# Decode attention with a gated MLP: the K and V loads move from SyncE's DMA queue to GpSimd's, each as a single packet for an engine

## Chip, core and metric

One NeuronCore of a Trainium2 chip runs the whole kernel in one launch. The metric is the device time of one execution in microseconds; lower is better. The core has five engines, which run their own instruction streams and meet at semaphores: TensorE (PE), VectorE (DVE), ScalarE (ACT), GpSimd (POOL) and SyncE (SP). Sixteen DMA engines move data between HBM and the on-chip memory (SBUF); SP, ACT and POOL can issue transfers to them.

## What is computed

One decode step for a batch of 4: layer norm, attention of one query against a cache of 8192 keys and values for each of 32 heads, then layer norm and a gated MLP, both with a residual.

```python
q = (layernorm(x) @ wq).reshape(B, 1, H, Dh)          # B=4, D=512, H=32, Dh=128
scores = einsum("bhqd,bhkd->bhqk", q, k_cache) * Dh ** -0.5
o = einsum("bhqk,bhkd->bhqd", softmax(scores), v_cache)   # Sk=8192
h = x + o.reshape(B, 1, H * Dh) @ wo
n = layernorm(h)
out = h + (sigmoid(n @ w_gate) * (n @ w_up)) @ w_down      # F=1792
```

All tensors are bf16. The K and V caches are 268 MB each, read once; everything else is small beside them.

## The kernel before

**Groups.** The 128 pairs of batch entry and head are worked on in NG = 32 groups of four heads of one batch entry. A group's K is one load of 128 partitions x 64 KB (8.4 MB), its V another. The tile KV has three slots of this size, through which 64 loads pass in turn: K0 in slot 0, K1 in slot 1, V0 in slot 2, K2 in slot 0, V1 in slot 1, K3 in slot 2 and so on.

**One group.** VectorE transposes K in place, in eight pieces (`transpose_k`, L332). TensorE multiplies each piece by the query vectors in Lq (`scores`, L342). VectorE and ScalarE make the softmax (`softmax`, L352 to L375); the step that closes the scores' use of K is the transpose at L357, and its token is `t_a5[g]`. TensorE then multiplies by V (`pv`, L385), one group later, and VectorE takes the result out of PSUM (`extract`, L412 to L415), two groups later, between the second and the third piece of the next transposes; its token is `t_ox[g]`. GpSimd has two small steps for each group: `fill_q` (L282) lays the next group's query vectors into Lq, and `keep_o` (L286) copies the result away. A group's first transpose waits for its K load, for `fill_q` and for the softmax step before.

**Loads and their waits.** `load_k(g)` waits for `t_ox[g-3]`, because its slot held V of group g-3; `load_v(g)` waits for `t_a5[g]`, because its slot held K of group g. The first ones differ: K0 waits for nothing, K1 for two matmuls on x (which lies in slot 1), K2 for `t_a5[0]`, and V0 for the projection of the queries (`t_qp`, L253), because slot 2 first holds the weight wq. All of these are issued by SyncE (L292 and L301, the last V at L299), in this order: wq (L181), K0, K1, V0, K2, V1, K3, V2 and so on, then the weights wo, w_gate, w_up (behind `t_a5[31]`) and w_down (behind the pv of group 30). x is loaded from ScalarE's queue (L180).

**The start.** wq has to land before the 128 matmuls at L253 can run; out of them come, through VectorE (L257, L269) and 16 small matmuls (L263), the query vectors, which `fill_q(0)` needs. GpSimd first clears and fills constants (L184 to L198).

**Loops and semaphores.** TensorE's and VectorE's streams are hardware loops of 10 turns over three groups each; ScalarE, GpSimd and SyncE run straight through. Inside the loops a wait must be on a constant, so these semaphores are counted down: a load adds 16 to `sl0` to `sl2` (K) or `v0` to `v2` (V), and the waiting engine subtracts 16 again (`take` in `emit`). The last V has a semaphore of its own, `vl`, that is only counted up. `fill` (L434) is work without a result that keeps TensorE's clock up in the last stage.

Of the kernel before, what the change touches and what calls it, by code (L numbers as in the profile page):

```python
# [11 lines left out]
class _Prog:  # L12
# [28 lines left out]
    def emit(self, eng, fn, waits=(), incs=1, key=None, take=(), keep=True):  # L41

        todo = self._waits(eng, waits)
        assert not (todo and self.looped), (eng, todo)
        key = key or eng
        tok = self.token(key, incs) if incs else None

        def run(e):
            for k, v in todo:
                e.wait_ge(self.sems[k], v)  # L50
            for k, v in take:
                e.wait_ge(self.sems[k], v).then_inc(self.sems[k], -v)  # L52
            made = fn(e)
            made = made if isinstance(made, list) else [made]
            if incs:
                assert len(made) == incs
                for m in made:
                    m.then_inc(self.sems[key], 1)

        if keep:  # L60
            self.ops[eng].append(run)
        return tok
# [26 lines left out]
def bass_sequential_preLN__mha_block_cached__glu_gated_glu__decode_kernel(  # L89
# [20 lines left out]
    SLOT = 4 * S * DH // 128  # L110
# [5 lines left out]
    prog = _Prog()  # L116
    emit = prog.emit

    with ExitStack() as es:
# [3 lines left out]
        def raw(t):  # L123
            return t.tensor if hasattr(t, "tensor") else t
# [31 lines left out]
        def kv(slot, off, inner, p0=0, np_=128):  # L156
            return bass.AP(raw(KV), p0 * KVROW + slot * SLOT + off, [[KVROW, np_], *inner])
# [10 lines left out]
        FY = (bank[1], FA)  # L168

        keys = ["sp", "act", "dve", "pool", "pe", "x", "out", "cs", "wq", "wo0", "wo1", "wg", "wu", "wd0", "wd1", "wd2", "wd3",  # L170
                "sl0", "sl1", "sl2", "vl", "v0", "v1", "v2", "tp", "pt", "ex", "dv", "sc", "pv", "lq"]
        for k in keys:
            prog.sems[k] = es.enter_context(nc.semaphore("s_" + k))

        dram_k = lambda g: A_k_cache[g % B, 4 * (g // B):4 * (g // B) + 4, :, :].rearrange(
            "h (p r) d -> (h p) (r d)", p=32)
        dram_v = lambda g: A_v_cache[g % B, 4 * (g // B):4 * (g // B) + 4, :, :].rearrange(
            "h (p r) d -> (h p) (r d)", p=32)
# [95 lines left out]
        t_v, t_et, t_pv, t_ox = {}, {}, {}, {}  # L274
        t_a5, t_oc = {}, {}

        def fill_q(g):
            m, b = g // B, g % B
            dst = bass.AP(raw(Lq), 15, [[4 * LW, 128], [LW, 4], [32, 4]])
            src = bass.AP(raw(q_all), m * 4 * B + b, [[128, 128], [B, 4], [0, 4]])  # L280
            msk = bass.AP(raw(mask), 0, [[4, 128], [0, 4], [1, 4]])
            emit("pool", lambda e: e.tensor_tensor(dst, src, msk, ALU.mult),  # L282
                 [t_q, t_mk, t_lq0, t_a5.get(g - 1), t_oc.get(g - 3)], key="lq")

        def keep_o(g):
            t_oc[g] = emit("pool", lambda e: e.tensor_copy(OT[:, g // B, :, g % B], OTs[:, g % 3, :]), [t_ox[g]])  # L286

        def load_k(g):
            i = max(2 * g - 1, 0)
            kslot[g] = slot = i % 3  # L290
            w = [] if g == 0 else [t_xT] if g == 1 else [t_a5[0]] if g == 2 else [t_ox[g - 3]]
            prog.dma("sp", f"sl{slot}", lambda e: e.dma_start(kv(slot, 0, [[1, SLOT]]), dram_k(g)), w)  # L292

        def load_v(g):
            last = g == NG - 1
            vslot[g] = slot = 0 if last else (2 * g + 2) % 3
            w = [t_ox[g - 2]] if last else [t_a5[g]] if g else [t_qp]
            if last:
                t_v[g] = [prog.dma("sp", "vl", lambda e: e.dma_start(kv(slot, 0, [[1, SLOT]]), dram_v(g)), w)] * 4  # L299
            else:  # L300
                t_v[g] = [prog.dma("sp", f"v{slot}", lambda e: e.dma_start(kv(slot, 0, [[1, SLOT]]), dram_v(g)), w)] * 4  # L301

        t_w = {}
        kslot, vslot = {}, {}
# [154 lines left out]
                return ins  # L459
            return emit("pe", f, waits)  # L460

        fill_q(0)
        load_k(0)
        load_k(1)
        load_v(0)
        TURNS = (NG - 2) // 3
        assert 2 + 3 * TURNS == NG
        for g in range(NG):
# [13 lines left out]
            if g > 1:  # L482
                keep_o(g - 2)
                if g + 1 < NG:
                    load_k(g + 1)
                else:
                    load_v(g)
# [3 lines left out]
            if 0 < g < NG - 1:  # L491
                load_v(g)
# [106 lines left out]
        def o_half(u):  # L599
# [3 lines left out]
        key, v = prog.dma("act", "out", lambda e: e.dma_start(  # L603
            out.rearrange("b s d -> (b s) d"), kv(0, 0, [[1, D]], 0, B)), [t_o])
# [33 lines left out]
```

## Time and profile before

| | |
|---|---|
| median of 3 runs | 1277.1 us (1276.98 to 1277.11) |
| the profiled execution | 1277.14 us, of which its span 1275.6 us |
| instructions in the span | 10932 |
| read from HBM | 550.77 MB, 432 GB/s over the span |
| granted TensorE clock, mean | 0.918 of full speed |

The profile records one execution. Times in its rows are microseconds from the start of the span. In a timeline row the first number is the start, the second the length; then follow engine, line of the kernel, operation, output<-inputs, the count of instructions merged into the row, and in brackets the idle time of the engine before it and what ended that. SPq and ACTq are the issue of a DMA by SyncE and ScalarE: the row's length is that of the issue, not of the transfer. A row with "KB" or a number after "x1," gives the time from the issue to the landing of the transfer. A row that begins with two times and a colon is one stretch: its length, the busy time and instruction count of PE, PE's weight loads, DVE, ACT and POOL, the granted clock, the DMA engines' busy share and GB/s. In a queue row stand its packets, megabytes and the time that they took as a share of 16 engines; q1 is SyncE's queue, q10 ScalarE's, and q8 and q14 fetch instructions.

### The profile page before, as it was taken

Reading aid. Unit: us, or ns where it says so; the run is one execution under the profiler, and the core shown is the slowest. Engines: PE = TensorE matmul, PEld = TensorE weight load, DVE = VectorE, ACT = ScalarE, POOL = GpSimd, SP = SyncE. Lnnn points to the kernel's source line nnn. Section 1 sums busy time; section 2 is a strip of 40 time slices with the busy share of each in tenths; the row PEclk is TensorE's granted clock in tenths of the full one; section 3 lists DMA queues with packets and bytes.
Section 4 is the critical chain, followed back from the end, with each engine's and each line's share of the span. In section 5 each row is a group of like instructions: output and inputs, shape, how many; then the busy total and the mean of one; then the engine's idle time right before and its main releaser. Section 6 shows DMA issues by size and latency. Waiting matters only on the chain. (4 is left out here: it accounts for less than half of the span.)

```text
span 1275.6 us, 10932 instructions
## 1 busy us (share of the span) xinstructions
PE 1001.2 (78%) x4450; PEld 409.7 (32%) x4450; DVE 701.8 (55%) x737; ACT 85.2 (7%) x202; POOL 22.6 (2%) x88
## 2 busy tenths in 40 slices
PE   1598777779777788777798777797777897777888
PEld 1233323333233333223333233333233332333334
DVE  0865665446655446654456654456554466544562
ACT  0000000000000000000000000000000000000010
POOL 1000000000000000000000000000000000000000
PEclk9899888899888898888998888998888998888989
DMA  9999999999999999999999999999999999999998
GB/s 420 434 425 434 427 444 432 430 438 427 442 434 430 438 427 444 432 432 436 427 444 432 432 436 434 438 432 434 434 434 438 432 436 432 436 436 430 440 430 371
DMA packets 10669, 550.95 MB, mean 432 GB/s; under 512 B 1176, under 2 KB 1440, under 8 KB 1824
## 3 DMA queue, kind: packets, MB, share of 16 engines
q1 hardware_dynamic: 10640, 550.77, 99.8%
q8 instruction: 8, 0.13, 0.0%
q14 instruction: 5, 0.04, 0.0%
q10 hardware_dynamic: 16, 0.01, 0.0%
HBM read 550.77 MB, written 0.00 MB: 432 GB/s over the span
## 5 line engine op out<-in xcount | busy, mean ns | idle before, releaser
L332 DVE STREAM_TRANSPOSE KV<-KV 128x2048 uint32<-128x2048 uint32 x256 | 568.6, 2279 | 379.1 <-DVEq L52 379.1
L342 PE MATMUL PS<-KV,Lq 128*128 128x512 bf16 x2048 | 543.6, 417 | 258.2 <-PEq L52 257.5
L385 PE MATMUL PS<-KV,PT 128*128 128x512 bf16 x1984 | 433.2, 379 | 0.0
L342 PEld LDWEIGHTS PS<-KV,Lq 128*128 128x128 bf16 x2048 | 199.8, 104 | 601.4 <-issue 442.7
L385 PEld LDWEIGHTS PS<-KV,PT 128*128 128x128 bf16 x1984 | 193.8, 98 | 234.5
L358 ACT ACTIVATE E_sb<-PS,TS 128x512 bf16<-128x512 f32 x32 | 22.0, 688 | 1124.6 <-DVE TS L357 1124.6
L352 DVE TENSOR_REDUCE TS<-PS 128x1 f32<-128x512 f32 x32 | 22.1, 692 | 70.4 <-DVEq L52 70.4
L369 ACT ACTIVATE PT<-ET 32x256 bf16<-32x256 bf16 x128 | 52.9, 413 | 30.8 <-DVE ET L361 28.5
L361 DVE STREAM_TRANSPOSE ET<-E_sb 128x512 bf16<-128x512 bf16 x32 | 22.8, 711 | 30.7 <-DVEq L52 30.7
L412 DVE STREAM_TRANSPOSE OX<-PS 128x512 f32<-128x512 f32 x31 | 20.9, 675 | 8.6 <-DVEq L52 8.6
L282 POOL TENSOR_TENSOR Lq<-q_all,mask 128x16 bf16<-128x16 bf16 x32 | 8.4, 263 | 575.0 <-DVE TS L357 563.4
L286 POOL COPY OT<-OTs 128x4 bf16<-128x4 bf16 x30 | 5.8, 192 | 622.3 <-DVE OTs L415 622.3
L434 PE MATMUL PS<-identf 128*128 128x512 f32 (+3 forms) x30 | 13.3, 551 | 0.0
L253 PE MATMUL PS<-xnT,KV 128*128 128x4 bf16 x128 | 3.6, 166 | 9.4 <-DMA KV<-in_A_wq_dram 9.4
L353 DVE STREAM_TRANSPOSE TS<-TS 128x32 f32<-128x32 f32 x32 | 6.8, 211 | 5.1 <-DVEq L52 0.6
L357 DVE STREAM_TRANSPOSE TS<-TS 128x32 f32<-128x32 f32 x32 | 6.8, 211 | 4.7
L374 DVE STREAM_TRANSPOSE TS<-TS 128x32 f32<-128x32 f32 x32 | 6.8, 211 | 4.7
L415 DVE TENSOR_SCALAR OTs<-Or,small 128x4 bf16<-128x4 f32 x30 | 6.9, 229 | 4.5 <-DVEq L52 1.4
L373 DVE COPY TS<-small 128x32 f32<-128x32 f32 x32 | 5.8, 182 | 6.2 <-DVEq L52 3.0
L355 DVE TENSOR_SCALAR TS<-small 128x32 f32<-128x32 f32 x32 | 5.8, 181 | 4.8 <-DVEq L52 0.2
L414 DVE TENSOR_REDUCE Or<-OX 128x4 f32<-128x16 f32 x31 | 5.6, 179 | 4.5
L354 DVE TENSOR_REDUCE small<-TS 128x1 f32<-128x16 f32 x32 | 5.4, 170 | 4.7
(87 smaller groups left out, 78.1 us busy)
## 6 DMA issues: line engine op xcount, KB each, us to landing
KV<-in_A_wq_dram SPq DMA_DIRECT2D x1, 4096.0 KB, 12.4
KV<-in_A_wo_dram SPq DMA_DIRECT2D x2, 2048.0 KB, 22.1
KV<-in_B_w_gate_dram SPq DMA_DIRECT2D x1, 1792.0 KB, 28.2
KV<-in_B_w_up_dram SPq DMA_DIRECT2D x1, 1792.0 KB, 32.0
KV<-in_B_w_down_dram SPq DMA_DIRECT2D x1, 1024.0 KB, 24.2
KV<-in_A_k_cache_dram SPq DMA_DIRECT2D x32, 32.4
KV<-in_A_v_cache_dram SPq DMA_DIRECT2D x32, 34.3
KV<-in_B_w_down_dram SPq DMA_DIRECT2D x1, 512.0 KB, 25.0
```

Of the source, the lines that this page charges most:

```text
L282: emit("pool", lambda e: e.tensor_tensor(dst, src, msk, ALU.mult), [t_q, t_mk, t_lq0, t_a5.get(g - 1), t_oc.get(g - 3)], key="lq")
L332: emit("dve", lambda e: e.transpose(v, v), key="tp", take=take, keep=keep)
L342: ins = e.matmul(S_b[0], Lq[:, hp, 15 - s:15 - s + 128], rhs, start=(s == 0 and hp == 0), stop=(s == NS - 1 and hp == 3))
L352: dv(lambda e: e.tensor_reduce(TS[:, 0, 0:1], S_b[0], AX.X, ALU.max), [t_ts0] if g == 0 else [], [("sc", 1)])
L353: dv(lambda e: e.transpose(TS[:, 1, :], TS[:, 0, :]))
L358: emit("act", lambda e: e.activation(E_sb[:, :], S_b[0], ACT.Exp, bias=TS[:, 3, 0:1], scale=SCALE, accum_out=TS[:, 4, 0:1]), [t_a5[g]], ke ...
L361: t_et[g] = dv(lambda e: e.transpose(ET[:, :], E_sb[:, :]), take=[("ex", 1)], key="dve")
L369: emit("act", lambda e, dst=dst, src=src: e.activation(dst, src, ACT.Copy), [t_et[g], t_pt0 if g < NG - 1 else t_ptl], key="pt")
L385: ins = e.matmul(O_b, PT[:, u3, off:off + 128], rhs, start=(j == 0 and rl == 0), stop=(j == 3 and rl == NS - 1))
L412: emit("dve", lambda e: e.transpose(OX[:, :, :].rearrange("p (r i) x -> p r i x", r=4), src), w, key="dv", take=take, keep=keep)
L415: t_ox[g] = emit("dve", lambda e: e.tensor_scalar(dst, Or[:, :], small[:, 2 + g % 3:3 + g % 3], None, op0=ALU.mult), take=[("dv", 1)], kee ...
L434: ins = e.matmul(bk[:, 0:cols], identf[:, :], bass.AP(raw(identf), 0, [[128, 128], [0, cols // 128], [1, 128]]), start=True, stop=True, sk ...
```

## The change

The K and V loads are issued by GpSimd, through a new helper `stream`, with `single_packet=True`. Each adds 16 to a new semaphore of its slot, `g0` to `g2`, that is only counted up. For each such load SyncE's stream gets a wait for that count, followed by an addition of 16 to the old semaphore, `sl` or `v`, which the loops count down as before. The last V adds to `vl` itself. The loads of x and of all weights stay where they were. In GpSimd's stream the order becomes: constants, K0, K1, `fill_q(0)`, V0, `fill_q(1)`, K2, `fill_q(2)`, V1, and then for each group `keep_o`, K, `fill_q`, V. SyncE's stream is wq, the waits, and the later weights. Nothing changes on TensorE, VectorE and ScalarE.

```diff
-                "sl0", "sl1", "sl2", "vl", "v0", "v1", "v2", ...
+                "sl0", "sl1", "sl2", "vl", "g0", "g1", "g2", "v0", "v1", "v2", ...
...
+        def stream(slot, key, src, w):
+            own = key if key == "vl" else f"g{slot}"
+            own, v = prog.dma("pool", own, lambda e: e.dma_start(
+                kv(slot, 0, [[1, SLOT]]), src, single_packet=True), w)
+            if own != key:
+                prog.ops["sp"].append(lambda e: e.wait_ge(prog.sems[own], v).then_inc(prog.sems[key], 16))
+            return own, v
+
         def load_k(g):
...
-            prog.dma("sp", f"sl{slot}", lambda e: e.dma_start(kv(slot, 0, [[1, SLOT]]), dram_k(g)), w)
+            stream(slot, f"sl{slot}", dram_k(g), w)
...
             if last:
-                t_v[g] = [prog.dma("sp", "vl", lambda e: e.dma_start(kv(slot, 0, [[1, SLOT]]), dram_v(g)), w)] * 4
+                t_v[g] = [stream(slot, "vl", dram_v(g), w)] * 4
             else:
-                t_v[g] = [prog.dma("sp", f"v{slot}", lambda e: e.dma_start(kv(slot, 0, [[1, SLOT]]), dram_v(g)), w)] * 4
+                stream(slot, f"v{slot}", dram_v(g), w)
...
-        fill_q(0)
         load_k(0)
         load_k(1)
+        fill_q(0)
         load_v(0)
```

More of the change, by code (lines that the diff above doesn't have):

```diff
@@ L170, in bass_sequential_preLN__mha_block_cached__glu_gated_glu__decode_kernel @@
         keys = ["sp", "act", "dve", "pool", "pe", "x", "out", "cs", "wq", "wo0", "wo1", "wg", "wu", "wd0", "wd1", "wd2", "wd3",
-                "sl0", "sl1", "sl2", "vl", "v0", "v1", "v2", "tp", "pt", "ex", "dv", "sc", "pv", "lq"]
+                "sl0", "sl1", "sl2", "vl", "g0", "g1", "g2", "v0", "v1", "v2", "tp", "pt", "ex", "dv", "sc", "pv", "lq"]
         for k in keys:
```

## The prediction

> **What bounds the kernel now.** I read the page's totals first, then the DMA queues, then one turn of the loop, then the two ends.
>
> ```profile
> span 1275.6 us, 10932 instructions
> PE 1001.2 (78%) x4450; PEld 409.7 (32%) x4450; DVE 701.8 (55%) x737; ACT 85.2 (7%) x202; POOL 22.6 (2%) x88
> DMA  9999999999999999999999999999999999999998
> q1 hardware_dynamic: 10640, 550.77, 99.8%
> ```
>
> No compute engine is busy over 78%, while one DMA queue keeps all 16 engines at work for 99.8% of the span. The next rows are one turn in the middle, group 16 or so: the totals of the turn, its DMA packets, the landing times of its two loads, and the instructions around their issue (start, length, engine, line).
>
> ```profile
> 600.00:638.62 38.62, 31.45 (x129) 12.81 (x128) 21.66 (x23) 2.43 (x6) 0.46 (x2) 0.90 1.00 434
> DMA packets 288, 16.78 MB, mean 435 GB/s; under 512 B 32, under 2 KB 32, under 8 KB 32
> q1 hardware_dynamic: 288, 16.78, 100.3%
> KV<-in_A_k_cache_dram SPq DMA_DIRECT2D x1, 32.5
> KV<-in_A_v_cache_dram SPq DMA_DIRECT2D x1, 34.3
> 600.08 13.27 DVE L332 STREAM_TRANSPOSE KV<-KV 128x2048 uint32<-128x2048 uint32 x6
> 600.20 0.33 SPq L292 DMA_DIRECT2D KV<-in_A_k_cache_dram  x1
> 600.24 0.19 POOL L286 COPY OT<-OTs 128x4 bf16<-128x4 bf16 x1 [20.91 <-DVE OTs L415]
> 617.63 0.33 SPq L301 DMA_DIRECT2D KV<-in_A_v_cache_dram  x1
> 617.69 0.26 POOL L282 TENSOR_TENSOR Lq<-q_all,mask 128x16 bf16<-128x16 bf16 x1 [17.26 <-DVE TS L357]
> ```
>
> Two loads, 16.78 MB, take 38.62 us, so one load is **19.31 us** of all 16 engines. It is 128 packets of 64 KB (256 of the 288; the 32 tiny ones are the landings), eight for each engine. K is issued at 600.20 and lands 32.5 us later, at 632.7, so its own data began near 632.7 - 19.3 = 613.4: it stood 13 us in the queue. V (617.63 + 34.3 = 651.9, begun near 632.6) stood 15. The queue never runs dry; in this stretch an issue may come 13 us later and cost nothing. The end hangs on the same queue:
>
> ```profile
> 1197.21 0.33 SPq L301 DMA_DIRECT2D KV<-in_A_v_cache_dram  x1
> 1235.82 0.80 SPq L312 DMA_DIRECT2D KV<-in_A_wo_dram  x2
> 1247.43 1.84 SPq L326 DMA_DIRECT2D KV<-in_B_w_down_dram  x4
> 1250.94 3.64 PE L399 MATMUL PS<-KV,PT 128*32 128x512 bf16 x64 [0.97 <-issue]
> KV<-in_B_w_down_dram SPq DMA_DIRECT2D x2, 128.0 KB, 24.7
> 1273.85 0.41 DVE L601 CAST KV<-PS 4x256 bf16<-4x256 f32 x1 [1.94 <-PE PS L591]
> ```
>
> The last pieces of w_down land 24.7 us after an issue that ends at 1249.27, near 1273, and the result is copied out at 1273.85. So the time is the DMA engines' work plus every microsecond in which they have nothing to do.
>
> **The change, part by part.** *Steady turns: nothing.* On POOL, K stands behind the L286 copy (ends 600.43 in place of an issue at 600.20) and V behind the L282 product (ends 617.95 for 617.63): 0.2 to 0.3 us, and whatever POOL needs to make descriptors, against 13 to 15 us of queue. POOL has the room: it is idle 20.91 and 17.26 us before those two. Behind a waiting V on POOL stand the next copy and K, both of which wait for a later event anyway. SP now waits for each landing and adds 16 to the old semaphore; a step of some 0.1 us (SP's issue at 617.63 and POOL's product at 617.69 follow one event and start 0.06 apart) on landings whose next data are already queued. SP's waits follow the order of issue, and behind the last of them stand only the weights, which wait until 1235.82 for another reason; V of group 30 (issued at 1197.21) lands after 34.3 us at 1231.5, 4 us before. The last V keeps its own semaphore and is not passed on. Were the cover gone, each late issue would cost its full lateness.
>
> *Packets: 0 to -4.0 us, I take -2.* Per engine, a load's eight packets become one. Rows with small and large packets bound what a packet costs:
>
> ```profile
> DMA packets 268, 3.86 MB, mean 429 GB/s; under 512 B 29, under 2 KB 29, under 8 KB 29
> DMA packets 2879, 167.71 MB, mean 434 GB/s; under 512 B 320, under 2 KB 320, under 8 KB 320
> ```
>
> The first is 1251 to 1260 (16 KB packets), the second 600 to 986.2 (64 KB). With a time per byte and a time c per packet, 16 x 9 = 144 engine-us and 16 x 386.2 = 6179 engine-us give c = 9 ns (scale the first by 167.71/3.86: 6257 engine-us with 11,644 packets; 77 more for 8,765 more). 64 loads x 7 packets x 9 ns = 4.0 us on every engine. The low end is 0, since records in the steady turn already fill 100.3% of the engines. No row decides, so I take the middle.
>
> *The start: +16 us.* Here K0 and K1 leave SP's queue, where they stood behind wq, for a queue of their own.
>
> ```profile
> 0.73 0.37 SPq L181 DMA_DIRECT2D KV<-in_A_wq_dram  x1
> 0.74 0.56 ACTq L180 DMA_DIRECT2D KV<-in_A_x_dram  x1
> 1.16 2.02 SPq L292 DMA_DIRECT2D KV<-in_A_k_cache_dram  x2
> 2.21 0.29 PE L229 MATMUL PS<-ident,KV 4*128 4x4 bf16 x4 [2.21 <-DMA KV<-in_A_x_dram]
> 5.96 0.32 POOL L198 MEMSET TS<- 128x256 f32 x1
> KV<-in_A_wq_dram SPq DMA_DIRECT2D x1, 4096.0 KB, 12.4
> 13.18 3.58 PE L253 MATMUL PS<-xnT,KV 128*128 128x4 bf16 x128 [9.38 <-DMA KV<-in_A_wq_dram]
> 16.79 0.33 SPq L301 DMA_DIRECT2D KV<-in_A_v_cache_dram  x1
> 17.89 0.26 POOL L282 TENSOR_TENSOR Lq<-q_all,mask 128x16 bf16<-128x16 bf16 x1 [11.61 <-DVE q_all L269]
> 33.66 17.66 DVE L332 STREAM_TRANSPOSE KV<-KV 128x2048 uint32<-128x2048 uint32 x8 [15.19 <-DVEq L52]
> ```
>
> wq lands at 0.73 + 12.4 = 13.13. The new K0 issue follows POOL's memsets, which end at 6.28; wq is then half done. What two queues do to each other these rows say in part:
>
> ```profile
> 1.00:2.00 1.00, 0.00 (x0) 0.00 (x0) 0.30 (x2) 0.66 (x1) 0.67 (x3) 1.00 1.40 365
> DMA packets 78, 2.56 MB, mean 426 GB/s; under 512 B 0, under 2 KB 0, under 8 KB 0
> q1 hardware_dynamic: 81, 5.31, 98.2%
> q8 instruction: 1, 0.02, 0.5%
> ```
>
> Data flow from some point between 1 and 2, so an SP issue needs about 1 us to its first packet. The second row is 4 to 10 us, wq alone: 32.8 KB a packet, 6 x 16 / 78 = 1.23 us each, eight for each engine. x, on ACT's queue, was used at 2.21 though wq had been issued before it: queues are served beside each other, not in order of issue. The last two rows are 17.5 to 30 us, inside K0: an instruction fetch got in between K0's 64 KB packets. So with K0 ready while wq runs, an engine turns from one to the other. How long a turn lasts no row shows; the ends are one 64 KB descriptor (38.62 / 16 = 2.41 us) and the eight that are now a single packet (19.31 us). I take the packet, the unit that the queue rows count.
>
> The Trainium skill (DMA: Bandwidth & Descriptors, Queues, rings and completion order) says that a DMA engine goes round its rings and drains a whole packet from one before it switches. By that rule the start costs what follows; by a turn of one descriptor it would cost nothing (rival 2).
>
> If wq still has two packets or more to go on any engine when K0's descriptors are there, that engine runs K0 (19.31), one packet of wq, K1 (19.31), the rest of wq. With its last two packets starting near 13.13 - 2 x 1.23 = 10.7, K0 has until then: 4.4 us after 6.28, of which an SP issue would need 1. I allow POOL 1.5 (bounds 1 and 3). wq then lands at 13.13 + 38.62 = **51.75**, with all K0 and K1 in and nothing else to load, since V0 needs wq's slot and stands behind the L282 product on POOL. That product ends 18.15 + 38.62 = 56.77; V0's data begin at 58.3: **idle 6.5**, and run to 77.6. DVE's first transposes need the product too: 56.8 in place of 33.66, all of groups 0 and 1 **23.2 later**.
>
> ```profile
> 55.65 0.33 SPq L292 DMA_DIRECT2D KV<-in_A_k_cache_dram  x1
> 55.70 0.26 POOL L282 TENSOR_TENSOR Lq<-q_all,mask 128x16 bf16<-128x16 bf16 x1 [37.55 <-DVE TS L357]
> 78.45 13.97 PE L385 MATMUL PS<-KV,PT 128*128 128x512 bf16 x64
> 81.31 0.26 POOL L282 TENSOR_TENSOR Lq<-q_all,mask 128x16 bf16<-128x16 bf16 x1 [25.35 <-DVE TS L357]
> ```
>
> K2, behind the product that ends at 55.96: issued 79.2, data from 80.7, **idle 3.1** after V0's 77.6; done 100.0. V1, behind the one that ends at 81.57: issued 104.8, data from 106.3, **idle 6.3**; done 125.6. K3 waits for pv(0), 78.45 + 13.97 + 23.2 = 115.6, and its extraction: 10 us of queue are left for that, and from there on the queue stays full. What is lost is never made up, since nothing later waits for anything but this queue. Sum: 6.5 + 3.1 + 6.3 = 15.9; less 2 for the packets, 13.9. The profiled execution took 1277.14 (1.5 around its span; the median is 1277.1): **1291**. With POOL at 1 or 3 us the three idles change by -1.5 or +4.5, and the packets by 2 either way: 1287.5 to 1297.6.
>
> **Rivals.** *1. No collision, not slower.* Were wq's queue served first, or did POOL need over 4.4 us for K0, so that at most one wq packet is left, wq would land at 13.1 or 32.4 and the product end by 37.5, before K1's data end near 51.7. No idle, only the packets' gain: 1277.1 - 2 = 1275, at best 1273. For it: the order of service between equal queues is not in any row. Against: x and the instruction fetch both got in.
>
> *2. The turn is one descriptor* (the single packet does not do what it says). wq has three or four packets left, each behind 2.41 us of K0: it lands near 13.13 + 4 x 2.41 = 22.8, V0 is issued by 28, still before 51.7. 1277.1.
>
> *3. Descriptors starve.* The Trainium skill (SBUF — State Buffer, SBUF: two separate sides) says that GpSimd cannot write descriptors while VectorE runs an operation that holds their shared ports. As a mechanism here: K would be issued after the six transposes, at 600.08 + 13.27 + 1.5 = 614.9, for a queue that runs dry at 613.4; 1.5 us idle in each of 29 turns, 43 us, so 1320. Against it speaks L286, which POOL ran at 600.24 in 0.19 us in the midst of those transposes; by that row the trap does not close here.
>
> **How the numbers follow.** Forecast 0.64; rival 1 0.12; rival 2 0.18; rival 3 or some other steady loss 0.06. Likeliest 1291, its own range 1287.5 to 1297.6; cases of both signs hold most of the chance, so the range is 1274 to 1298, which leaves out about 0.1. About 0.2% (2.6 us) is what a measurement of this kernel can tell from no change. Faster needs rival 1 with the packets at their upper end, or a gain no row shows: 0.09. Same is rival 2 and most of rival 1: 0.25. Slower: 0.66.
>
> **What would show it.** Right: PE's L253 starts near 52, not 13; DVE's first transposes near 57; the DMA row has dips near 55, 79 and 103 and nowhere else in the middle; a turn still takes 38.5 or so, and the three early loads start as above. Packets: steady turns shorter than 38.62 by up to 0.12. Wrong: L253 near 13 to 23 (rivals 1 and 2, told apart by its exact start), DVE's transposes starting later turn after turn with DMA gaps (rival 3), or a turn longer than 38.7 with the DMA busy throughout, for which I have no term.

## Result and the profile after

| | before | after |
|---|---|---|
| median | 1277.11 us (1276.98 to 1277.2, 6 runs) | 1281.97 us (1281.5 to 1283.17, 6 runs) |
| profiled execution, of which span | 1277.14, 1275.6 us | 1282.0, 1280.2 us |

The change makes the kernel slower: the ratio is 1.0039, with a 95% interval of 1.0026 to 1.0052. That is 4.9 us, in the forecast direction but about a third of the forecast 13.9 us, and the place is another one.

The first rows are the page of the kernel after: its span, its DMA row in 40 slices and its queues.

```profile
span 1280.2 us, 10995 instructions
DMA  9999999999999999999999999999999999999997
q0 software_dynamic: 9216, 536.88, 96.8%
q1 hardware_dynamic: 1424, 13.89, 2.6%
```

K and V now go through q0, GpSimd's queue; wq and the late weights stay on q1. There is no dip in the early slices, where the forecast had three; only the last slice falls, from 8 to 7. The start is the next view, the timeline after:

```profile
6.22 1.20 POOL L290 DMA_DIRECT2D KV<-in_A_k_cache_dram  x2
20.10 3.58 PE L253 MATMUL PS<-xnT,KV 128*128 128x4 bf16 x128 [16.30 <-DMA KV<-in_A_wq_dram]
24.80 0.26 POOL L282 TENSOR_TENSOR Lq<-q_all,mask 128x16 bf16<-128x16 bf16 x1 [17.38 <-DVE q_all L269]
25.02 0.59 POOL L290 DMA_DIRECT2D KV<-in_A_v_cache_dram  x1
33.74 17.66 DVE L340 STREAM_TRANSPOSE KV<-KV 128x2048 uint32<-128x2048 uint32 x8 [8.36 <-DVEq L52]
55.95 0.59 POOL L290 DMA_DIRECT2D KV<-in_A_k_cache_dram  x1
81.56 0.59 POOL L290 DMA_DIRECT2D KV<-in_A_v_cache_dram  x1
```

wq lands 6.9 us later than before (L253 at 20.10 for 13.18), but the first transposes start at 33.74 for 33.66: K0's last byte, not the query vectors, still sets them. K2 and V1 are issued 0.3 us later than before, into a queue that is full. The start costs nothing. In the middle, the same turn as in the prediction:

```profile
600.00:638.62 38.62, 30.33 (x130) 12.30 (x129) 21.68 (x22) 2.43 (x6) 1.41 (x4) 0.94 1.00 434
q0 software_dynamic: 288, 16.78, 100.3%
KV<-in_A_k_cache_dram POOLq DMA_DIRECT2D x1, 32.2
KV<-in_A_v_cache_dram POOLq DMA_DIRECT2D x1, 34.1
600.18 13.27 DVE L340 STREAM_TRANSPOSE KV<-KV 128x2048 uint32<-128x2048 uint32 x6
600.47 0.53 POOL L290 DMA_DIRECT2D KV<-in_A_k_cache_dram  x1
```

434 GB/s and 288 packets, as before. Each load is issued some 0.3 us later and lands that much sooner after its issue. The whole loss lies in the last 45 us:

```profile
1218.67 0.53 POOL L290 DMA_DIRECT2D KV<-in_A_v_cache_dram  x1
1235.94 0.81 SPq L320 DMA_DIRECT2D KV<-in_A_wo_dram  x2
1247.35 2.74 PE L442 MATMUL PS<-identf 128*128 128x512 f32 x6
1254.04 5.32 PE L407 MATMUL PS<-KV,PT 128*32 128x512 bf16 x64 [3.94 <-issue]
1278.48 0.41 DVE L609 CAST KV<-PS 4x256 bf16<-4x256 f32 x1 [1.82 <-PE PS L599]
```

The last PV (L407, L399 before) is the first work that needs the last V. It starts at 1254.04 for 1250.94, **3.10 us late**, and takes 5.32 us for 3.64, **1.68 more**: 4.78, against a longer span of 4.6. From its end to the last copy everything takes as long as before, within 0.2 us. Why the V is late stands in the queue rows of 1239 to 1251.5, and why the PV is long in two windows (the granted clock is the third number from the end):

```profile
DMA packets 135, 5.24 MB, mean 419 GB/s; under 512 B 4, under 2 KB 4, under 8 KB 4
q0 software_dynamic: 67, 4.13, 76.5%
q1 hardware_dynamic: 67, 1.10, 20.5%
...
1254.00:1257.00 3.00, 2.96 (x40) 1.50 (x44) 0.00 (x0) 0.00 (x0) 0.00 (x0) 0.72 1.01 431
1257.00:1260.00 3.00, 3.00 (x42) 1.51 (x34) 0.59 (x1) 0.00 (x0) 0.00 (x0) 0.71 1.00 428
```

While the last V is on its way in q0, 67 packets of the weights go out of q1, one for each packet of q0 (63 of these are V's of 64 KB, 4.13 MB; the four under 512 B are landings). In the kernel before, the weights stood behind V in the same queue. Its queue row of 1239 to 1248 has the same 63 packets of V with no other load beside them, and its window of 1255 to 1260 has the full clock:

```profile
q1 hardware_dynamic: 63, 4.13, 106.2%
...
1255.00:1260.00 5.00, 4.39 (x29) 1.66 (x28) 1.79 (x7) 0.00 (x0) 0.00 (x0) 1.00 1.01 431
```

67 packets over 16 engines are four or five on each; at 1.10 MB / 67 = 16 KB a packet takes a quarter of 2.41, 0.6 us, so by this estimate V's last packet is put off by 2.4 to 3.0 us, and the slowest engine counts. Then TensorE, which has stood idle for 3.94 us, runs at a lower granted clock: 0.72 and 0.71 of full speed in windows that had 1.0 before.

### The profile page after: what moved, and what is told of

Its sections match the earlier page's. It is cut to its first block, busy times and chain, and to the rows that moved or that the text cites. A ratio compares the mean times of both kernels' runs of the same rounds, so it can differ in the third digit from the quotient of the medians.

```text
span 1280.2 us, 10995 instructions
## 1 busy us (share of the span) xinstructions
PE 1003.5 (78%) x4450; PEld 410.0 (32%) x4450; DVE 701.8 (55%) x737; ACT 85.1 (7%) x202; POOL 53.4 (4%) x152
## 5 line engine op out<-in xcount | busy, mean ns | idle before, releaser
L369 DVE STREAM_TRANSPOSE ET<-E_sb 128x512 bf16<-128x512 bf16 x32 | 22.8, 711 | 30.7 <-DVEq L52 30.7
L290 POOL DMA_DIRECT2D KV<-in_A_v_cache_dram x32 | 18.9, 589 | 0.0
L290 POOL DMA_DIRECT2D KV<-in_A_k_cache_dram x32 | 17.1, 534 | 0.0
L253 PE MATMUL PS<-xnT,KV 128*128 128x4 bf16 x128 | 3.6, 166 | 16.3 <-DMA KV<-in_A_wq_dram 16.3
```

Source lines behind the costliest of these rows:

```text
L290: own, v = prog.dma("pool", own, lambda e: e.dma_start(kv(slot, 0, [[1, SLOT]]), src, single_packet=True), w)
L369: t_et[g] = dv(lambda e: e.transpose(ET[:, :], E_sb[:, :]), take=[("ex", 1)], key="dve")
```

## The experiments

**The weights in V's queue.** All late weights are issued by GpSimd.

```diff
-                t_w[f"wo{i}"] = prog.dma("sp", f"wo{i}", ...
+                t_w[f"wo{i}"] = prog.dma("pool", f"wo{i}", ...
```

(and the same for w_gate, w_up and w_down)

> The changed kernel with wo, w_gate, w_up and w_down issued by GpSimd too, so that the last V and the weights stand in one queue again. Theory A (the 4.9 us come from the weights on SyncE's queue taking turns with the last V on GpSimd's): the last V lands near 1251, the last PV starts there and takes 3.6 us, time 1277 to 1278. Theory B (a load that GpSimd issues lands later by itself): the last V still lands near 1254, time 1281 to 1282.

```profile
1250.89 3.64 PE L407 MATMUL PS<-KV,PT 128*32 128x512 bf16 x64 [0.92 <-issue]
```

Measured: 1276.97 us (1276.83 to 1277.08), ratio to before 0.9998 (0.9989 to 1.0008). The row is from the timeline of this run: start and length of the last PV are those of the kernel before. All of the loss is gone with the second queue at the end, although every K, V and late weight is still issued by GpSimd and SyncE still passes the landings on. So those two parts of the change cost nothing that can be measured, and theory B falls.

**The weights later.** On SyncE's queue still, but not before the PV of group 30 is done.

```diff
-            w = [t_a5[NG - 1]]
+            w = [t_pv[NG - 2]]
```

> The changed kernel with wo, w_gate and w_up held back on SyncE's queue until the PV of group 30 is done (near 1247.5 in place of 1236), when the last V has one 64 KB packet or so left on each engine. Theory A (turns): the last V lands within 1 us of 1251, no DMA gap, time 1277 to 1278.5. Theory B (GpSimd's loads land later by themselves): the last V lands near 1254, time 1281 to 1282.

```profile
1247.64 3.41 SPq L320 DMA_DIRECT2D KV<-in_A_wo_dram  x2
1251.05 3.64 PE L407 MATMUL PS<-KV,PT 128*32 128x512 bf16 x64 [0.87 <-issue]
...
PEld PS L465 <- DMA KV<-in_A_wo_dram: 1.8, 1, 1.8
PEld PS L568 <- DMA KV<-in_B_w_up_dram: 1.0, 1, 1.0
```

Measured: 1278.17 us (1277.44 to 1279.26), ratio 1.0009 (0.9999 to 1.0018). The last V is in time again, with GpSimd's queue and SyncE's as in the change, so it is the overlap of the two queues in time that matters. The remaining 1 us, hardly clear of the noise, has moved: the last two rows, from this run's list of waits, have the projection and the MLP wait 1.8 us for wo and 1.0 for w_up, where the kernel before waits 0.8 for each.

**No flag.** The changed kernel without `single_packet=True`.

```diff
-                kv(slot, 0, [[1, SLOT]]), src, single_packet=True), w)
+                kv(slot, 0, [[1, SLOT]]), src), w)
```

> The changed kernel without single_packet=True. If the flag makes neither longer turns nor cheaper packets here (what the interleaving of wq and K0 by single 64 KB packets says): wq lands near 20, the last V near 1254, time 1282 as with it (1281.5 to 1282.5). If the flag does something at the end of the run or to the rate, the time moves by more than 0.5 us.

Measured: 1281.65 us (1281.43 to 1283.08), ratio 1.0039 (1.0025 to 1.0053), the change's own ratio. The last PV starts at 1254.03. wq landed earlier than in the profile of the change (L253 at 17.68 for 20.10), but the run with longer turns below, which has the flag, shows 17.84, so this difference is not the flag's.

**The flag alone.** The kernel before, K and V still on SyncE's queue, with the flag.

```diff
-            prog.dma("sp", f"sl{slot}", lambda e: e.dma_start(kv(slot, 0, [[1, SLOT]]), dram_k(g)), w)
+            prog.dma("sp", f"sl{slot}", lambda e: e.dma_start(kv(slot, 0, [[1, SLOT]]), dram_k(g), single_packet=True), w)
```

(and the same at the two V loads)

> The kernel before with single_packet=True on the K and V loads, still issued by SyncE. The prediction's term for cheaper packets says 0 to -4 us, so 1273 to 1277; if a 64 KB packet costs the same merged or not: 1277.1 within 0.3, and a turn of two loads stays at 38.63.

Measured: 1277.18 us (1277.02 to 1277.3), ratio 1.0 (0.999 to 1.001); the turn from 600 to 638.62 still holds 288 packets and 16.78 MB. The flag changes neither the packets that the profile counts nor the time: that term of the sum is 0, not -2.

**TensorE kept busy.** The changed kernel with more filling work ahead of the last PV.

```diff
-        fill(3, S_b[0], [t_et[NG - 1]])
+        fill(7, S_b[0], [t_et[NG - 1]])
```

> The changed kernel with seven instead of three filling matmuls ahead of the last PV (some 6.4 us of TensorE work in place of 2.7, from 1247.4 to 1253.8), so that TensorE does not stand idle for 3.9 us before it. If the idle time is what halved the granted clock for 3.4 us and made the last PV 5.32 us long: the PV takes 3.6 us again, no half clock after 1250, time 1280.3 (1279.9 to 1280.7). If the clock has nothing to do with it: 1282.

```profile
1250.00:1254.00 4.00, 3.51 (x9) 1.24 (x7) 0.00 (x0) 0.00 (x0) 0.46 (x2) 1.00 0.88 377
1254.00:1257.00 3.00, 2.97 (x56) 1.70 (x60) 0.00 (x0) 0.00 (x0) 0.00 (x0) 1.00 0.99 426
1257.00:1260.00 3.00, 3.00 (x33) 1.26 (x22) 1.67 (x6) 0.00 (x0) 0.00 (x0) 1.00 0.98 420
1254.03 3.64 PE L407 MATMUL PS<-KV,PT 128*32 128x512 bf16 x64 [0.53 <-issue]
```

Measured: 1280.19 us (1279.79 to 1280.84), 1.8 below the change. The rows are this run's windows and the last PV in its timeline: it starts as late as in the change, at full clock, and takes 3.64 us again. So of the 4.9 us some 1.8 are the clock and 3.0 (1280.19 - 1277.16, the kernel before beside it) the late V.

**Longer turns.** The changed kernel with wo as one load of 32 KB rows; its rows lie in another order than the projection reads them.

```diff
-            for i in range(2):
-                t_w[f"wo{i}"] = prog.dma("sp", f"wo{i}", lambda e, i=i: e.dma_start(
-                    kv(1, i * 16 * D, [[1, 16 * D]]),
-                    A_wo[2048 * i:2048 * (i + 1), :].rearrange("(p k) f -> p (k f)", k=16)), w)
+            t_w["wo0"] = t_w["wo1"] = prog.dma("sp", "wo0", lambda e: e.dma_start(
+                kv(1, 0, [[1, 32 * D]]), A_wo.rearrange("(p k) f -> p (k f)", k=32)), w)
```

> The changed kernel with wo as one load of 32 KB rows in place of two with 16 KB rows, so that each turn of the weights' queue takes 1.21 us in place of 0.61 (wo's rows then lie in another order than the projection reads them). If the engines go turn by turn, one packet of each queue: the last V, which has four or five packets left on each engine when wo starts, is held up by 4.9 to 6 us in place of 2.4 to 3 and lands near 1256.5 to 1257, time 1284 to 1286. If the two queues share bytes evenly or the lateness is GpSimd's own: it lands at 1254 as before, time 1282.

```profile
q0 software_dynamic: 68, 4.19, 64.7%
q1 hardware_dynamic: 71, 2.33, 35.9%
...
1256.97 5.04 PE L405 MATMUL PS<-KV,PT 128*32 128x512 bf16 x64 [6.90 <-issue]
```

Measured: 1284.99 us (1284.68 to 1285.61), ratio 1.0063 (1.0046 to 1.008). The first rows are this run's queues from 1239 to 1254: about as many packets of the weights as of V's queue, 71 to 68 (64 of V and four landings), now of 32 KB. The PV starts 6.0 us later than in the kernel before, twice the 3.1. The engines share turns, not bytes, and a turn is one packet in the profile's sense.

**K0 and K1 behind wq.** The changed kernel with these two loads on SyncE's queue.

```diff
-            stream(slot, f"sl{slot}", dram_k(g), w)
+            if g < 2:
+                prog.dma("sp", f"sl{slot}", lambda e: e.dma_start(kv(slot, 0, [[1, SLOT]]), dram_k(g)), w)
+            else:
+                stream(slot, f"sl{slot}", dram_k(g), w)
```

> The changed kernel with K0 and K1 issued by SyncE again, behind wq. If the start costs nothing (the trace has the first transposes at 33.74 against 33.66): wq lands at 13.1 in place of 20.1, and the time stays at 1282 (1281.5 to 1282.5). If the late wq cost something that came out later: down to 1280 or 1281.

```profile
17.84 0.72 POOL L290 DMA_DIRECT2D KV<-in_A_v_cache_dram  x1
45.79 17.66 DVE L343 STREAM_TRANSPOSE KV<-KV 128x2048 uint32<-128x2048 uint32 x8 [27.59 <-DVEq L52]
95.02 0.59 POOL L290 DMA_DIRECT2D KV<-in_A_v_cache_dram  x1
...
60.00:88.00 28.00, 17.63 (x70) 6.64 (x67) 22.01 (x21) 2.43 (x6) 0.75 (x2) 0.82 1.04 447
90.00:96.00 6.00, 5.75 (x27) 2.65 (x28) 1.83 (x7) 0.78 (x2) 0.75 (x2) 1.00 0.02 4
```

A miss: 1289.4 us (1288.2 to 1289.94), ratio 1.0097 (1.008 to 1.0114), 7.4 above the change. The expectation looked at wq and forgot V0. wq lands early (L253 at 12.91), so V0 is issued at 17.84, into the other queue, and takes turns with K0. The rows show what follows: K0 lands 12 us later, all of group 0 moves by as much, V1 can only be issued at 95.02, and the DMA engines, done with what they had by 89, move 4 GB/s from 90 to 96. This is the chain that the prediction worked out for wq, with V0 as the intruder and 7 us idle in place of 16.

**A hardware queue with the flag.** The kernel before with K0 and K1 issued by ScalarE, flag set.

```diff
-            prog.dma("sp", f"sl{slot}", lambda e: e.dma_start(kv(slot, 0, [[1, SLOT]]), dram_k(g)), w)
+            prog.dma("act" if g < 2 else "sp", f"sl{slot}", lambda e: e.dma_start(
+                kv(slot, 0, [[1, SLOT]]), dram_k(g), single_packet=g < 2), w)
```

> The kernel before with K0 and K1 issued by ScalarE, with single_packet=True, some 4 us into wq. It asks the prediction's question of a hardware queue: turns of one 64 KB packet land wq near 13 + 5 x 2.4 = 25 and leave the time at 1277 to 1277.5; turns of a whole load land it near 52, with the three idle stretches that the prediction worked out, and a time of 1290 to 1295.

```profile
4.87 0.84 ACTq L292 DMA_DIRECT2D KV<-in_A_k_cache_dram  x2
22.84 3.57 PE L253 MATMUL PS<-xnT,KV 128*128 128x4 bf16 x128 [18.61 <-DMA KV<-in_A_wq_dram]
36.31 17.66 DVE L333 STREAM_TRANSPOSE KV<-KV 128x2048 uint32<-128x2048 uint32 x8 [8.19 <-DVEq L52]
75.06 17.66 DVE L333 STREAM_TRANSPOSE KV<-KV 128x2048 uint32<-128x2048 uint32 x8 [13.71 <-DVEq L52]
89.50:98.00 8.50, 7.92 (x37) 3.27 (x35) 4.69 (x7) 0.57 (x1) 0.26 (x1) 1.00 0.01 3
```

Half a hit: wq lands near 23, as turns of one 64 KB packet have it, and not near 52; but the time is 1286.66 us (1286.36 to 1286.92), ratio 1.0074 (1.0057 to 1.009). V0, here on SyncE's queue at 26.43, takes turns with K1 on ScalarE's: group 1's transposes start at 75.06 for 58.90 in the kernel before, V1 is issued at 97.42 for 81.26, and the same hole opens, 8.5 us with 3 GB/s.

## Why the prediction was right or wrong

*What bounds the kernel, and the steady turns: right.* The rate, the turn and the landing times are those of before, and the run with all of K, V and the late weights on GpSimd's queue is as fast as the kernel before. SyncE's passing on is within that.

*Packets, -2: wrong, 0.* The flag alone moves nothing: no packets were merged as the profile counts them. Whether a packet costs 9 ns is therefore not tested.

*The start, +16: wrong at one step*, "I take the packet, the unit that the queue rows count". With that word I gave a whole load of 19.31 us one turn. The trace has 288 packets in a turn with the flag and without it, and the turns were of that size: wq landed near 20, not 51.75. K0 did come while wq had a packet or two left on each engine (22 of its 32 KB packets start after 10 us); so it is the turn's length that failed, not the collision. The collision itself came about narrowly: the 1.5 us allowed for GpSimd (bounds 1 and 3) were too short, since the first packet of its queue runs 3.8 us after the issue at 6.22, and the latest moment that the forecast had worked out was 10.7. Rival 2 named this outcome and gave its landing, near 22.8, and its cost, none. The Trainium skill's rule (DMA: Bandwidth & Descriptors, Queues, rings and completion order), turns of a packet, agrees with the runs if one 64 KB descriptor is the packet, and not with the 9 to 17 descriptors that it calls typical of one; that the flag would make the packet longer no run here shows, in either kind of queue.

*The end: a term that was missing.* The prediction set the late weights against SyncE's own order, "behind the last of them stand only the weights, which wait until 1235.82 for another reason", and stopped there. It did not ask what they would meet on the DMA engines: in the kernel before they stood behind the last V, in the changed one beside it. The mechanism was on the table, two queues that take turns, and was applied to one end of the kernel only. Measured: 3.0 us for the late V and 1.8 for the clock. Nothing covers a late landing there, because no load is left behind which it could hide, and the chain from the last PV to the output has a fixed length. That the kernel came out slower, as forecast, is therefore luck: the loss that was forecast is not there, and the one that is there was not forecast.

*Rival 1* fell at its premise: the queues do share. *Rival 3* fell as argued: GpSimd's issue at 600.47 takes 0.53 us inside the six transposes that start at 600.18, so the trap of which the Trainium skill warns (SBUF — State Buffer, SBUF: two separate sides) does not close for these transposes.

## What to carry to other kernels

A transfer that moves to another queue loses its place in line: list every transfer that stood before or behind it, at both ends of the kernel, and ask which of them now runs beside it. Where the DMA engines are the bound, sharing changes no total, but it can make the load that is needed first as late as the one that is not; the single queue in the order of need was 5 to 12 us faster here than the arrangements in which a K, a V or the weights ran beside a load that was needed sooner. If a wait of some microseconds ahead of TensorE's last stage can't be avoided, fill it, since the clock may drop behind it.

## What the runs showed of the hardware

- The 16 DMA engines take turns between queues by single packets: 64 KB of V against 16 KB or 32 KB of the weights, 63 to 67 and 64 to 71 in the stretches shown. `single_packet=True` made no difference that the packet counts, the interleaving or the times show, on GpSimd's, SyncE's or ScalarE's queue.
- A load in a queue of its own reached busy engines late. GpSimd's first was issued at 6.22, and no packet of its queue runs before 10. This is not GpSimd's alone: in the changed kernel SyncE's wo, issued at 1235.94, has no packet before 1239.3; in the last run ScalarE's K0, issued at 4.87, has none before 8, and SyncE's V0, issued at 26.43, none before 31. Into empty DMA engines GpSimd's load of 95.02 in the K0-and-K1 run moved data from 96.3, 1.3 us later; SyncE's of 97.42 in the last run from 98.35, 0.9 later. What the 3 to 5 us are spent on is open.

```profile
DMA packets 58, 1.90 MB, mean 475 GB/s; under 512 B 0, under 2 KB 0, under 8 KB 0
q1 hardware_dynamic: 58, 1.90, 110.3%
```

These two rows are the changed kernel from 6 to 10 us: q1 alone, no q0.

- An idle stretch of 3.9 us halved TensorE's clock in the changed kernel (0.50 from 1256 to 1258), and one as long did not in the run with K0 and K1 on SyncE's queue:

```profile
1261.88 3.64 PE L410 MATMUL PS<-KV,PT 128*32 128x512 bf16 x64 [3.89 <-issue]
```

The Trainium skill (TensorE: Matmul & The Clock Gate, Part 1: The HAM clock gate) has a free-running window of about 3.4 us decide, and lets the clock fall after an idle one. The length agrees: in the changed kernel the clock falls at 1255.3 and is back 3.4 us later. That the whole window must be idle does not: the 3.4 us before that fall hold 1.3 us of the PV. In the other run, windows counted on from a fall at 1218.9 part the idle time near 1259.9 into two stretches of 1.9 and 2.0 us, and the clock stays. So a window's share of work may decide; two cases do not prove it.

- SyncE's four issues of w_down took 6.07 us after the change, with two queues under way, for 1.84 before. They took 5.92 to 8.01 us in every run in which they were issued while V and the weights shared the engines, and 1.84 in the runs with all of these on SyncE's queue. They lie off the path there, and the cause is open.

```profile
1247.55 6.07 SPq L334 DMA_DIRECT2D KV<-in_B_w_down_dram  x4
```
